# A kernel of attention and a Fourier layer: TensorE's operands at the right end of SBUF, helper tiles at the left, products with V in four blocks

## The chip, the cores and the metric

The kernel runs on one core of one Trainium2 chip. Its engines run side by side, each through its own list of instructions: TensorE (PE in the profile; PEld is its loading of weights, the stationary operand), VectorE (DVE), ScalarE (ACT), GpSimd (POOL), and SyncE (SP), which here issues every DMA. They wait for one another through semaphores. SBUF holds the tiles, PSUM the products of TensorE.

The metric is the time of one execution on the device in microseconds. Before the change it was 3028.86 us, the median of three runs (3026.84 to 3029.26).

## The reference, cut to what matters

Two layers on inputs of 2048 rows and 1024 columns, in float32; the results stand side by side in the output.

```python
def _A_ref(x, wqkv, wo):
    B, S, D = x.shape
    H = 32; Dh = D // H
    qkv = (x @ wqkv).reshape(B, S, 3, H, Dh).transpose(2, 0, 3, 1, 4)
    q, k, v = qkv[0], qkv[1], qkv[2]
    scores = jnp.einsum("bhqd,bhkd->bhqk", q, k) * Dh ** -0.5
    p = softmax(scores, axis=-1)
    o = jnp.einsum("bhqk,bhkd->bhqd", p, v)
    return o.transpose(0, 2, 1, 3).reshape(B, S, D) @ wo

def _B_ref(x, dft_seq_re, dft_seq_im, dft_hid_re, dft_hid_im):
    a = jnp.einsum("bsd,ed->bse", x, dft_hid_re)
    b = jnp.einsum("bsd,ed->bse", x, dft_hid_im)
    return jnp.einsum("ts,bse->bte", dft_seq_re, a) - jnp.einsum("ts,bse->bte", dft_seq_im, b)
```

## The kernel before, in words

**Dense products.** The products with wqkv, the two Fourier products and the one with wo (`qkv`, `dense1`, `dense2`, `project`) are each split in two by two blocks and done with seven block products instead of eight, from sums and differences of blocks. Each float32 operand is split into a high part (a cast, `halves`, L447 on VectorE or L445 on ScalarE) and the rest (a subtraction, L450), and three products (high with high, low with high, high with low) give one product's precision. So every dense product is a group of 12 or 24 matmuls at L361 in `group`, all in a type that TensorE takes in one pass. The stationary operand is a `piece` (tiles h and l) or, in `project` and in the V steps of `qkv`, a slot; the moving one is a slot of two halves of 512 columns (`moving`). What comes from memory lands in tiles raw and g (er in the early steps), is added up there (L425) and then split. A result is gathered from PSUM by VectorE, into a sum (an accumulator from `accs`, also a slot) or into tile e, and stored. Tile c brings back a stored partial result.

**Attention.** Head by head. `scores` computes q times k with 96 rows (L1162, 64 matmuls a head, out to psS), takes the row maximum on VectorE (L1168) and the exponential with its sum on ScalarE (L1171). `transposed` computes the transposed scores with 98 rows, the two extra carrying the row minimum of the negated maxima (L1285, 64 a head, out to psT), and ScalarE writes their exponentials into one of 27 tiles pt (L1289). Products with V (L1304) take the pt tiles of several key tiles at once, four column blocks of the array side by side; they are plain float32, two matmul instructions each. Up to which key tile a block of them goes is in ENDS: (0, 6, 11, 16), three blocks a head. `gather_o` (L1315, L1317) adds the blocks up, `result` scales them by tile rt and stores them.

**The order.** A planner written in the kernel (`Plan`) simulates the engines with fixed costs in microseconds and writes the order of all instructions out; the chip then keeps it. TensorE takes work of three streams of attention, S (L1162), T (L1285) and V (L1304), when it is ready, and otherwise a fill, the next matmul of a dense product. A fill goes ahead of attention only where the share of fills done lags behind the share of attention done (L1417, with RES fills held back). A product with V waits up to PATIENCE while other attention work is about to be ready or ScalarE has less than STOCK of work queued (L1392 to L1397). MM, PV and SWITCH are the planner's costs of a matmul, of one key tile in L1304 and of one switch to L1304 and back.

**Where tiles lie.** SBUF is allotted as two stacks that grow towards each other, one from the left end, the lowest addresses, and one from the right. Before the change:

- right: pool `big`, 20 slots of 4 KiB (0 to 19; the sums are 0 to 3 and 12 to 15 in the Fourier part), and pool `pre`, 21 tiles of 2 KiB (h, l, raw, g, e, c)
- left, one after another: `qk0` (qs0, ks0: q and k of even heads), `sm` (small tiles of the softmax), then `v` (early steps: er, sums of qkv, slots 28 to 31, vh, stage), which `att()` replaces by `att` (qs1, ks1, vt, qx, 27 pt, rt, ot), which `op_pool()` replaces by `op` (projection: slots 20 to 27, raw, g and kept tiles)

A pool allots its tiles in the order of their first use. Work that uses a pool's place after another waits for the last users of the former; `att_gate` collects the last work of the early qkv steps, and `behind` that of attention.

## Time and profile before

| | |
|---|---|
| median of three runs | 3028.86 us |
| the profiled execution | 3029.23 us |
| its span, first to last instruction | 3027.3 us |
| TensorE busy | 3002.2 us, 99% |
| VectorE busy | 2403.0 us, 79% |
| ScalarE busy | 2279.5 us, 75% |
| GpSimd busy | 849.6 us, 28% |
| granted TensorE clock, mean | 0.998 |

The profile records one execution. Busy times are from records of each instruction; a line such as `L361` is the line of the kernel. A group line gives the engine, the operation, what is written and read, shapes, how many there were, busy time and mean duration, then the idle time before them and what ended it. In a timeline each line has a start in us from the beginning of the span and a length; equal neighbours are merged with their count. Matmuls overlap in their pipeline and their ends are modelled, so the time that one costs is the distance between starts. A window line gives, for a stretch of time, the busy time and number of instructions of each engine asked for, the granted clock, the busy share of the DMA engines and GB/s.

### The profile page before, as it was taken

How to read it: one execution, taken by the hardware profiler on the slowest of the kernel's cores; microseconds unless marked ns; L12 is line 12 of the kernel's file. 1: busy time of each engine (PE TensorE's matmuls, PEld its weight loads, DVE VectorE, ACT ScalarE, POOL GpSimd, SP SyncE). 2: the span in 40 equal slices, each digit the busy share in tenths (PEclk: the TensorE clock that was granted, in tenths of full speed). 3: DMA queues.
4: the chain of work that ended last, by engine and by line, in shares of the span. 5: the costliest groups of instructions: out<-in, count | busy, mean ns of one | idle time of the engine just before them, and what ended most of it. 6: DMA issues, size and time to landing. Idle time of an engine off the chain costs nothing.

```text
span 3027.3 us, 45365 instructions
## 1 busy us (share of the span) xinstructions
PE 3002.2 (99%) x14912; PEld 2151.6 (71%) x14912; DVE 2403.0 (79%) x3243; ACT 2279.5 (75%) x4312; POOL 849.6 (28%) x631
## 2 busy tenths in 40 slices
PE   9999999999999999999999999999999999999999
PEld 7887666677677666777777666666666766776787
DVE  7778889788877877787777788887777789787896
ACT  4348888888888888888888788888888888885221
POOL 2313335132212321221112343332211254240142
PEclk9999999999999999999999999999999999999999
DMA  9975658666625644554535675555433586556852
GB/s 341 351 224 165 203 177 278 206 229 222 198 77 175 204 126 138 180 181 137 157 91 153 216 237 165 162 154 161 128 105 101 160 261 214 150 171 203 296 183 94
DMA packets 376313, 558.06 MB, mean 184 GB/s; under 512 B 110896, under 2 KB 110896, under 8 KB 376016
## 3 DMA queue, kind: packets, MB, share of 16 engines
q1 hardware_dynamic: 376080, 555.17, 57.6%
q8 instruction: 120, 1.97, 0.3%
q14 instruction: 113, 0.93, 0.1%
HBM read 401.93 MB, written 153.09 MB: 183 GB/s over the span
## 4 chain that ended last, share of the span: by engine, by line
PE 81%; DVE 3%; ACT 1%; DMA 1%; issue 1%; SPq 0%; DVEq 0%; ACTq 0%
PE pd L361 36%; PE psT L1285 15%; PE pd L1304 14%; PE psS L1162 14%; PE psT L361 3%; DVE negm L1168 1%; ACT psS L1171 1%; DVE raw L425 0%; DVE h L447 0%; DMA raw<-o_d 0%; DVE slot L447 0%; ACT pt L1289 0%; DMA out<-e 0%; DMA c<-u_d 0%; DMA g<-in_wd 0%
## 5 line engine op out<-in xcount | busy, mean ns | idle before, releaser
L1289 ACT ACTIVATE pt<-psT 128x512 f32<-128x512 f32 x2048 | 1178.0, 654 | 386.2 <-PE psT L1285 385.1
L1168 DVE TENSOR_REDUCE negm<-psS 128x1 f32<-128x1024 f32 x1024 | 1240.3, 1220 | 209.8 <-PE psS L1162 205.0
L1171 ACT ACTIVATE psS<-psS,negm 128x1024 f32<-128x1024 f32 x1024 | 1174.3, 1147 | 77.2 <-DVE negm L1168 73.2
L361 PE MATMUL pd<-slot,h 128*128 128x512 f32 x3352 | 1152.7, 394 | 0.0
L1285 PE MATMUL psT<-qs,ks 98*128 98x512 f32 x2048 | 816.3, 402 | 1.1 <-ACT pt L1289 1.1
L361 PEld LDWEIGHTS pd<-slot,h 128*128 128x128 f32 x3352 | 634.2, 189 | 141.9 <-issue 0.8
L361 PE MATMUL pd<-slot,l 128*128 128x512 f32 x1676 | 660.2, 394 | 0.5 <-DVE l L450 0.5
L1285 PEld LDWEIGHTS psT<-qs,ks 98*128 98x128 f32 x2048 | 385.1, 189 | 178.4 <-issue 74.6
L1162 PE MATMUL psS<-ks,qs 96*128 96x512 f32 x1552 | 482.0, 397 | 11.2 <-ACT psS L1171 9.5
L1304 PE MATMUL pd<-pt,vt 128*32 128x512 f32 x4096 | 462.1, 597 | 1.7 <-DVE slot L598 1.2
L450 POOL TENSOR_TENSOR l<-raw,h 128x512 fp32r<-128x512 f32 x150 | 201.4, 1343 | 902.6 <-DVE h L447 419.9
L425 POOL TENSOR_TENSOR raw<-raw,g 128x512 f32<-128x512 f32 x214 | 285.8, 1341 | 469.8 <-DMA raw<-in_ct 115.8
L361 PEld LDWEIGHTS pd<-slot,l 128*128 128x128 f32 x1676 | 317.3, 189 | 71.3 <-DVE l L450 0.9
L1162 PEld LDWEIGHTS psS<-ks,qs 96*128 96x128 f32 x1552 | 290.7, 189 | 86.2 <-ACT psS L1171 21.0
L1304 PEld LDWEIGHTS pd<-pt,vt 128*32 128x32 f32 x4096 | 123.5, 110 | 288.1 <-issue 270.3
L450 POOL TENSOR_TENSOR slot<-raw,slot 128x512 fp32r<-128x512 f32 x145 | 203.4, 1410 | 368.6 <-DVE slot L447 232.7
L1171 ACT ACTIVATION_READ_ACCUMULATOR psS<-psS,negm 128x1 f32 x1024 | 270.8, 264 | 0.0
L361 PE MATMUL pd<-slot,slot 128*128 128x512 f32 x768 | 195.5, 394 | 0.0
L361 PEld LDWEIGHTS pd<-slot,slot 128*128 128x128 f32 x768 | 144.4, 188 | 32.9
L447 DVE CAST h<-raw 128x512 fp32r<-128x512 f32 x321 | 153.2, 478 | 15.7 <-PE pd L361 13.5
L1162 PE MATMUL psS<-ks,qx 96*128 96x512 f32 x496 | 151.9, 397 | 0.3
L425 DVE TENSOR_TENSOR raw<-raw,g 128x512 f32<-128x512 f32 x158 | 121.8, 776 | 33.2 <-DMA raw<-in_ct 9.8
(116 smaller groups left out, 1852.1 us busy)
## 6 DMA issues: line engine op xcount, KB each, us to landing
raw<-in_ct SPq DMA_DIRECT2D x224, 256.0 KB
g<-in_ct SPq DMA_DIRECT2D x128, 256.0 KB
qk_d<-e SPq DMA_DIRECT2D x52, 512.0 KB
qs<-qk_d SPq DMA_DIRECT2D x128, 192.0 KB
ks<-qk_d SPq DMA_DIRECT2D x128, 192.0 KB
raw<-ab_d SPq DMA_DIRECT2D x96, 256.0 KB
c<-u_d SPq DMA_DIRECT2D x88, 256.0 KB
g<-ab_d SPq DMA_DIRECT2D x80, 256.0 KB
```

What stands on the lines that cost most here:

```text
L361: nc.tensor.matmul(box["ps"], a[1]((a[0].hi, a[0].lo)[u]()), b[1]((b[0].hi, b[0].lo)[v]()), start=k == 0, stop=k == n - 1)
L425: (nc.gpsimd if e == "POOL" else nc.vector).tensor_tensor(out=dest(), in0=dest() if a is None else a.get(), in1=other["q"] if "q" in other ...
L447: nc.vector.tensor_copy(hi(), raw())
L450: (nc.gpsimd if e == "POOL" else nc.vector).tensor_tensor(out=lo(), in0=raw(), in1=f(hi()), op=ALU.subtract)
L1162: nc.tensor.matmul(p[:, i * NB : i * NB + NB], (qx["t"] if own else QS[h % 2][0:96])[:, qt * P : qt * P + P], KS[h % 2][0:96, c * 1024 + i ...
L1168: nc.vector.tensor_reduce(out=ST["negm"][:, c, qt : qt + 1], in_=box["p"], axis=AX.X, op=ALU.max, negate=True)
L1171: nc.scalar.activation(box["p"], box["p"], AF.Exp, bias=ST["negm"][:, c, qt : qt + 1], accum_out=ST["sums"][:, c, qt : qt + 1])
L1285: nc.tensor.matmul(box["p"], KS[h % 2][0:98, t * P : t * P + P], QS[h % 2][0:98, j * NB : j * NB + NB], start=True, stop=True)
L1289: nc.scalar.activation(box["t"], box["p"], AF.Exp)
L1304: nc.tensor.matmul(po["p"][j * DH : j * DH + DH, :], VT[h][:, k, :], box["t"], start=(k == t0), stop=(k == t), tile_position=(0, j * DH),)
```

## The change

The slots and pools are dealt out anew, and the products with V are cut into four blocks.

- Right now: `big` with slots 0 to 11 alone, a new pool `parts` (h and l), `qk0`, in the early steps a pool `vh` (slots 28 to 39), in attention `att` (qs1, ks1, qx and 22 of the 27 pt), in the projection `oph` (slots 20 to 27).
- Left now: `pre` (raw, g, e, c), `sm`, in the early steps `v` (er, sums of qkv, the tiles vh, stage), from attention on `sums` (slots 12 to 19) with `atl` (5 of the pt, vt, rt, ot) above it, and `op` (raw, g, kept tiles) in the place of `atl`.
- The slots of moving tiles form a ring of 0 to 11 in place of 16 to 19 and 4 to 11; sums are 16 to 19 and 12 to 15. In the last two qkv steps the V weights and the x tiles have changed places between slots 0 to 3 and 16 to 19. Slots 12 to 19 come free with `att_gate`.
- ENDS is (0, 4, 8, 12, 16); MM, PV and SWITCH, RES and PATIENCE have other values; the small exponential of `sums` is worked in place (tile ww is gone).

```diff
-ENDS = (0, 6, 11, 16)
+NLOW = 5
+ENDS = (0, 4, 8, 12, 16)
...
     def slot(i, shape, dt=F32R):
-        if i >= 20:
-            return (vp if i >= 28 else op_pool()).tile(shape, dt, name=f"slot{i}")
-        return big.tile(shape, dt, name=f"slot{i}", tag=f"slot{i}")
-
-    pre = ctx.enter_context(tc.tile_pool(name="pre", bufs=1, side="right", reuse_waits="tile"))
+        if i < 12:
+            return big.tile(shape, dt, name=f"slot{i}", tag=f"slot{i}")
+        if i < 20:
+            att()
+            return late["sums"].tile(shape, dt, name=f"slot{i}", tag=f"slot{i}")
+        if i < 28:
+            op_pool()
+            return late["oph"].tile(shape, dt, name=f"slot{i}")
+        return vph.tile(shape, dt, name=f"slot{i}")
...
+    parts = ctx.enter_context(tc.tile_pool(name="parts", bufs=1, side="right", reuse_waits="tile"))
+    pre = ctx.enter_context(tc.tile_pool(name="pre", bufs=1, reuse_waits="tile"))
...
-    qk0 = tc.alloc_tile_pool(name="qk0", bufs=1)
+    qk0 = tc.alloc_tile_pool(name="qk0", bufs=1, side="right")
...
+    vph = tc.alloc_tile_pool(name="vh", bufs=1, side="right", reuse_waits="tile")
...
             vp.release()
-            late["att"] = a = tc.alloc_tile_pool(name="att", bufs=1, reuse_waits="tile")
+            vph.release()
+            late["sums"] = ctx.enter_context(tc.tile_pool(name="sums", bufs=1, reuse_waits="tile"))
+            late["atl"] = tc.alloc_tile_pool(name="atl", bufs=1, reuse_waits="tile")
+            late["att"] = a = tc.alloc_tile_pool(name="att", bufs=1, side="right", reuse_waits="tile")
...
-    AROUND, SUMS = (16, 17, 18, 19, 4, 5, 6, 7, 8, 9, 10, 11), (0, 1, 2, 3, 12, 13, 14, 15)
+    SUMS = (16, 17, 18, 19, 12, 13, 14, 15)
...
-    MM, PV, SWITCH, TINY = 0.234, 0.786, 0.515, 0.17
+    MM, PV, SWITCH, TINY = 0.229, 0.866, 0.19, 0.17
...
-    RES = 600
+    RES = 400
...
-    PATIENCE = 2.0
+    PATIENCE = 0.5
...
-                    box[key] = pre.tile([P, 4, P], F32R, name=key, tag=key, bufs=3)
+                    box[key] = parts.tile([P, 4, P], F32R, name=key, tag=key, bufs=3)
...
                 i = 8 * ((x + 1) % 2) + k
+                i = i if i < 12 else 20 + i
             else:
-                i = (8 * (x - 5) + k) % 12 if x < 11 or k < 4 else 8 + k
+                i = (8 * (x - 5) + k) % 12 if x < 11 else (16, 8)[k // 4] + k
...
-            WV[x, c] = moving((28 if x in (1, 3) else 12 if x == 10 else 16) + c, ...)
+            WV[x, c] = moving((28 if x in (1, 3) else 12 if x == 10 else 0 if x == 11 else 36) + c, ...)
...
                 for u in ahead[0].users + slots[28:]:
                     att_gate.extend(u)
+                for i in range(12, 20):
+                    slots[i] = list(att_gate)
...
-            B[x][n] = moving(AROUND[(8 * x + n) % 12], b_terms(p, n), ...)
+            B[x][n] = moving((8 * x + n) % 12, b_terms(p, n), ...)
...
         WHERE = {
-            1: ([16, 20], 0), 7: ([4, 8], 24), 2: ([0, 4], 20), 6: ([8, 0], 24),
-            5: ([4, 8], 20), 3: ([0, 4], 24), 4: ([8, 0], 20),
+            1: ([20, 24], 0), 7: ([4, 8], 20), 2: ([0, 4], 24), 6: ([8, 0], 20),
+            5: ([4, 8], 24), 3: ([0, 4], 20), 4: ([8, 0], 24),
         }
...
-            box["w"] = sm.tile([P, 2, NS], F32, name="ww", bufs=1)
-            nc.scalar.activation(box["w"], box["t"], AF.Exp)
+            nc.scalar.activation(box["t"], box["t"], AF.Exp)
...
+                here = pt_r.n % NPT < NLOW
...
-                    box["t"] = att().tile([P, NB], F32, name="pt", bufs=NPT)
+                    box["t"] = att_low().tile([P, NB], F32, name="ptl", bufs=NLOW) if here else att().tile([P, NB], F32, name="pt", bufs=NPT - NLOW)
```

30 lines of the change are left out of this document (17 added, 13 removed).

## The prediction

> **What bounds the kernel now.** I read the page first, engines and granted clock.
>
> ```profile
> span 3027.3 us, 45365 instructions
> PE 3002.2 (99%) x14912; PEld 2151.6 (71%) x14912; DVE 2403.0 (79%) x3243; ACT 2279.5 (75%) x4312; POOL 849.6 (28%) x631
> PEclk9999999999999999999999999999999999999999
> PE 81%; DVE 3%; ACT 1%; DMA 1%; issue 1%; SPq 0%; DVEq 0%; ACTq 0%
> ```
>
> TensorE is never without work, its clock is whole, and the chain that ended last is its own. So the question is how long one matmul takes, and whether anything slower hides behind TensorE. Busy time of a pipelined matmul doesn't tell that; starts do. In the timeline of the output projection (L361), the first product has its moving operand in slots 0 to 3 throughout; its stationary one lies in slots 16 to 19 (right stack) for four groups of 12, then in slots 20 to 23 (left stack).
>
> ```profile
> 2869.41 5.60 PE L361 MATMUL pd<-slot,slot 128*128 128x512 f32 x24
> 2874.85 5.68 PE L361 MATMUL psT<-slot,slot 128*128 128x512 f32 x24
> 2880.37 5.76 PE L361 MATMUL pd<-slot,slot 128*128 128x512 f32 x24
> 2885.97 5.76 PE L361 MATMUL psT<-slot,slot 128*128 128x512 f32 x24
> ```
>
> From start to start, the 24 with both operands on the right take 5.44 us, 226.7 ns each; the 24 with the weights on the left take 5.60 us, 233.3 each. Shape, moving tile and neighbours are the same: 6.6 ns go with where the weights lie. Two stretches without products with V, one of attention and one of the Fourier part alone behind it (windows of time: matmuls, weight loads, VectorE, ScalarE, GpSimd, granted clock, DMA share, GB/s):
>
> ```profile
> 815.42:841.47 26.05, 26.05 (x113) 21.17 (x112) 22.13 (x27) 25.31 (x48) 1.30 (x1) 1.00 0.35 96
> 2818.25:2849.56 31.31, 31.31 (x140) 25.90 (x138) 27.73 (x47) 7.54 (x12) 5.39 (x3) 1.00 0.86 311
> ```
>
> A window also counts one or two matmuls that run into it, so the first is 112 in 26.05 us, 232.6 ns, and the second 138 in 31.31 us, 226.9. In the second all operands (slots, h, l) lie on the right, while DMA is at 0.86 and VectorE at 27.73 of 31.31 us: traffic of others isn't what slows a matmul. In the first, 98-row (L1285) and 96-row (L1162) matmuls read qs, ks and qx from the left stack. Even few of these slow their neighbours; early, in a stream of fills from the right:
>
> ```profile
> 210.00 0.63 PE L1162 MATMUL psS<-ks,qs 96*128 96x512 f32 x2
> 210.47 0.40 PE L361 MATMUL pd<-slot,h 128*128 128x512 f32 x1
> 210.71 0.39 PE L361 MATMUL pd<-slot,l 128*128 128x512 f32 x1
> 210.94 0.62 PE L361 MATMUL pd<-slot,h 128*128 128x512 f32 x2
> 211.40 0.63 PE L1162 MATMUL psS<-ks,qs 96*128 96x512 f32 x2
> ```
>
> Two from the left and four from the right take 1.40 us, 233.3 each: one pair costs all six. So I read a step, not a sum: 226.7 where a stream reads from the right alone, about 233 where it touches the left.
>
> The second thing seen in the attention window is ScalarE: 25.31 of 26.05 us. Between products with V, attention goes at ScalarE's pace and the fills (Fourier and projection products) take what TensorE has left. A faster matmul alone doesn't shorten attention; it lets more fills run inside it.
>
> **The change, part by part.** *Placement.* How many matmuls change regime: windows by source line, attention from the first L1285 to the last product with V, and the end.
>
> ```profile
> 248.29:2817.90 2569.61, 1440.75 (x4869) 1.00 0.56 174
> 2880.37:3027.30 146.93, 142.97 (x613) 1.00 0.39 132
> ...
> 248.29:2817.90 2569.61, 816.34 (x2048) 1.00 0.56 174
> ...
> 71.68:248.29 176.61, 22.64 (x72) 1.00 0.76 260
> 248.29:2817.90 2569.61, 611.28 (x1976) 1.00 0.56 174
> ```
>
> (First two L361, the third L1285, the last two L1162.) Attention: 4869 + 2048 + 1976 = 8893 matmuls times 232.6 - 226.8 = 5.8 ns: 51.6 us. Projection: 613 x 6.6 ns = 4.0 us; its left slots become a right pool. Before attention: two V steps of 96 matmuls with slots 28 to 31 on the left, 1.3 us, and 36 pairs of L1162 that each hold back six, 36 x 6 x 6.6 ns = 1.4 us. What newly reads from the left are the last two steps of qkv, whose moving V weights (slots 12 to 15) and x tiles (16 to 19, 12 to 15) fall into the new left pool of sums: 8 + 8 + 16 groups of 12, 384 x 6.6 ns = 2.5 us back. Sum: 51.6 + 4.0 + 1.3 + 1.4 - 2.5 = 55.8 us off TensorE. No row shows a 96- or 98-row matmul reading from the right, so this has two ends: only the 128-row streams gain (5.3 us), or all do (55.8); I take the upper one, because a 128-row matmul shows the same 233 when its operand lies on the left.
>
> *Products with V in four blocks.* From 96 blocks of five or six key tiles to 128 of four.
>
> ```profile
> 2746.80 0.39 PE L361 MATMUL pd<-slot,h 128*128 128x512 f32 x1
> 2747.12 4.50 PE L1304 MATMUL pd<-pt,vt 128*32 128x512 f32 x40
> 2751.55 0.73 PE L1285 MATMUL psT<-qs,ks 98*128 98x512 f32 x2
> 2752.12 0.40 PE L361 MATMUL pd<-slot,h 128*128 128x512 f32 x1
> ...
> 2771.30 5.36 PE L1304 MATMUL pd<-pt,vt 128*32 128x512 f32 x48
> 2776.59 0.73 PE L1285 MATMUL psT<-qs,ks 98*128 98x512 f32 x2
> ```
>
> Five tiles hold TensorE 4.43 us, six 5.29: 0.86 a tile and 0.13 fixed. The entry takes 0.32 instead of 0.23, the two matmuls behind it 0.57 instead of 0.46. So a block costs 0.33 us beside its tiles, and 32 more cost 10.6 us on TensorE. Each brings one more add on VectorE:
>
> ```profile
> L1317 DVE TENSOR_TENSOR ot<-ot,pd 128x512 f32<-128x512 f32 x64 | 43.9, 687 | 122.3 <-PE pd L1304 122.1
> L598 DVE TENSOR_TENSOR slot<-slot,pd 128x512 f32<-128x512 f32 x12 | 8.2, 679 | 0.9 <-PE pd L361 0.8
> L598 DVE TENSOR_TENSOR acc<-acc,pd 128x512 f32<-128x512 f32 x10 | 6.8, 681 | 5.9 <-PE pd L361 5.7
> ```
>
> 32 x 0.687 = 22 us more on an engine with some 600 us idle: hidden while fills and scores go on in the other banks; uncovered it is at most 22 us. The lower two rows are the same add on the right (slot) and on the left (acc): 2 ns apart, so sums and raw tiles cost VectorE nothing on the left, and I put 0 there.
>
> The shorter block matters to ScalarE, which starves while one runs.
>
> ```profile
> ACT pt L1289 <- PE psT L1285: 385.1, 232, 6.0
> ```
>
> 385.1 us over 96 blocks is 4.0 each. A mean block with its entry is 16 x 0.86 / 3 + 0.13 + 0.32 = 5.04 us, one of four tiles 3.89; with the same stock of queued exponentials the starving falls by 1.15 to 2.85, and 128 x 2.85 = 365: attention becomes some 18 us shorter than its 2569.61.
>
> *The rest.* The share of fills held back (RES) and its slower rule don't bind: TensorE already ran ahead of that share, since fills fill whatever attention leaves. The new gate on slots 12 to 19 makes the first sum of the later qkv steps wait for the last early store; four free banks and the first scores lie over it, and I put 0, with 5 us if they don't cover it. DMA issues on SP keep number and size; exchanging slots 0 to 3 for 16 to 19 moves none past another. Working the small exponential in place removes no instruction. The planner's costs for a matmul, a tile of V and a switch decide the order alone; a plan nearer to 227 ns moves waits about, for which I allow the 2 us below.
>
> *Sum.* TensorE: 3029.23 - 55.8 + 10.6 = 2984.0. The profiled execution (3029.23) is 0.4 above the median 3028.86, which I neglect. Against it stands the end of attention:
>
> ```profile
> 2819.75 0.33 SPq L1334 DMA_DIRECT2D o_d<-ot  x1
> 2824.14 0.38 SPq L409 DMA_DIRECT2D raw<-in_wo  x1
> ...
> 2827.60 0.63 ACT L445 ACTIVATE slot<-raw 128x512 fp32r<-128x512 f32 x1 [16.83 <-DMA raw<-in_wo]
> ...
> 2866.69 2.88 PE L361 MATMUL psT<-slot,slot 128*128 128x512 f32 x12
> ...
> 3020.37 2.96 PE L361 MATMUL psT<-slot,slot 128*128 128x512 f32 x12
> ```
>
> Now 48.8 us of fills cover the way from the last product with V (2817.9) to the projection (2866.69). The saved time uses those up inside attention. The bare way is some 14 us by these rows (store, first weight load to cast 10 us, a few loads more). With 672 matmuls at 226.7 (152.3) and the tail behind the last (3027.3 - 3020.37 - 2.8 = 4.1) an attention of the old length ends at 2817.9 + 170.4 = 2988.3, 2990 with what lies around the span; 18 us shorter, it no longer binds. I take TensorE's sum and 2 us for waits that a faster TensorE meets: **2986 us**.
>
> **The rivals.**
>
> *Part of it stays left of the border.* On the right stack the rows show the fast regime down to 122 KiB from its end (20 slots of 4, 21 tiles of 2 KiB). After the change the stack is 138 KiB deep, and qs1 and ks1, allotted first in their pool, may lie lowest: 16 KiB that no row shows fast. If the border lies above them, odd heads stay slow, and L1285 of one head is mixed with L1162 of the next, so one of the two is always odd; the pair above spoils its six. Then between none and half of the 51.6 us comes: 3034 to 3009, nearer the former, 3028. For it: the unseen 16 KiB. Against: none of the fast rows weakens towards its low end (h and l lie lowest, 226.9).
>
> *Place does nothing for L1285 and L1162*; their row counts make the 233. Only 4.0 + 1.3 us come, and 10.6 are paid: 3034.5. Against it: the 128-row rows. The Trainium skill's page "SBUF — State Buffer" (Who interferes with whom) says that PE never waits on anyone and knows waits only at the port that VectorE and GpSimd share; by that rule placement is worth 0 altogether and the time would be 3029.2 + 10.6 = 3039.8. The trace disagrees, 226.7 against 233.3, so this has no chance beyond the rival's own.
>
> *ScalarE starves, slower.* The patience before a product with V falls from 2.0 to 0.5 us: a block may start before exponentials are queued, ScalarE loses up to 1.5 us a block, and fills run out before attention ends. It decides once attention ends later than 3027.3 - 170.4 = 2856.9, 57 us behind the 2800 expected, 0.44 us a block. With half of the 1.5: 2800 + 96 + 170.4 = 3066, 3068 with the rest. For it: 25.31 of 26.05. Against: with 16 of 27 exponential tiles in a block instead of 24, L1285 has eleven free ones to run ahead, so the stock refills itself.
>
> **How the numbers follow.** Forecast 0.70; border 0.12; place does nothing 0.06; starving 0.12. The forecast's own range is 2970 (attention and waits both shrink) to 3002 (attention not shorter, gate and added adds partly open). To leave out no more than 2 in 10 the range must take in the first two rivals: 2970 to 3036. A measurement tells 0.2%, 6 us. Faster: 0.70 and 0.04 of the border's 0.12: 0.74. Same: 0.05 of the border and 0.03 of the second: 0.08. Slower: the rest, 0.18.
>
> **What would show it.** Attention windows at about 227 ns a matmul for placement, odd and even heads alike; if the border is the cause, L1285 keeps two durations. L1304 in blocks of 32 holding about 3.57 us. ScalarE's wait for psT L1285 near 365 us; over 440 speaks for starving, with idle TensorE before the projection. Fewer than some 60 fills between the last product with V and the projection. It is wrong if matmuls stay at 232, or if TensorE falls below 98%.

## The result and the profile after

The changed kernel takes 3037.17 us (median of 7 runs, 3035.80 to 3040.12), the kernel before in the same runs 3029.26 (7 runs, 3026.84 to 3031.91). The ratio is 1.0026, with an interval from 1.0014 to 1.0038: slower by a quarter of a per cent. The forecast was 2986.

The page of the kernel changed: span, busy times, granted clock, and the engines' shares of the chain that ended last.

```profile
span 3034.8 us, 45369 instructions
PE 3010.0 (99%) x14912; PEld 2149.4 (71%) x14912; DVE 2435.1 (80%) x3283; ACT 2293.7 (76%) x4316; POOL 840.5 (28%) x619
PEclk9999999999999999999999999999999999999999
PE 92%; DVE 5%; ACT 1%; DMA 1%; issue 1%; POOL 0%; SPq 0%; ACTq 0%; DVEq 0%; POOLq 0%
```

TensorE still sets the end and its clock is whole in all 40 slices of the page, so the time must be looked for in the distance between matmuls again. The lines of the code have moved: L361 is L380 here, L1285 L1308, L1162 L1185, L1304 L1327, L1317 L1340, L1289 L1312. The timeline of the projection, all of whose operands lie on the right now (start, length, line, operation):

```profile
2881.04 5.60 PE L380 MATMUL pd<-slot,slot 128*128 128x512 f32 x24
2886.48 5.60 PE L380 MATMUL psT<-slot,slot 128*128 128x512 f32 x24
2891.92 5.60 PE L380 MATMUL pd<-slot,slot 128*128 128x512 f32 x24
```

Every 24 take 5.44 us, 226.7 ns each, where those with weights on the left had taken 5.60. That is what was expected. Two stretches of the attention without products with V, windows of time as before (matmuls, weight loads, VectorE, ScalarE, GpSimd, granted clock, DMA share, GB/s):

```profile
1228.95:1246.41 17.46, 17.46 (x76) 14.19 (x75) 16.84 (x23) 16.80 (x32) 9.40 (x7) 1.00 0.94 287
2561.48:2577.77 16.29, 16.29 (x71) 13.24 (x70) 15.85 (x20) 14.21 (x27) 9.32 (x7) 1.00 0.65 204
```

Both windows begin and end at a start, with one more matmul that runs into them: 75 in 17.46 us and 70 in 16.29 us are 232.8 and 232.7 ns. Nothing has been gained in the attention, although qs, ks, qx, h, l and the slots all lie on the right. The early fills with a pair of scores among them, in the timeline:

```profile
209.66 0.63 PE L1185 MATMUL psS<-ks,qs 96*128 96x512 f32 x2
210.12 0.39 PE L380 MATMUL pd<-slot,h 128*128 128x512 f32 x1
210.36 0.40 PE L380 MATMUL psT<-slot,h 128*128 128x512 f32 x1
210.59 0.40 PE L380 MATMUL psT<-slot,l 128*128 128x512 f32 x1
210.82 0.62 PE L380 MATMUL psT<-slot,h 128*128 128x512 f32 x2
211.28 0.40 PE L380 MATMUL psT<-slot,l 128*128 128x512 f32 x1
211.52 0.63 PE L1185 MATMUL psS<-ks,qs 96*128 96x512 f32 x2
```

Eight matmuls in 1.86 us, 232.5 each, with nothing read from the left. The pair still holds up its neighbours. What sets it apart from them is now its 96 rows alone.

A block of products with V in the timeline, one of 32 matmuls, with its entry and what follows it:

```profile
1543.81 0.39 PE L1308 MATMUL psT<-qs,ks 98*128 98x512 f32 x1
1544.13 3.64 PE L1327 MATMUL pd<-pt,vt 128*32 128x512 f32 x32
1547.70 0.73 PE L1308 MATMUL psT<-qs,ks 98*128 98x512 f32 x2
1548.27 1.09 PE L1185 MATMUL psS<-ks,qx 96*128 96x512 f32 x4
```

The add behind each block, among the costliest groups (busy time and mean ns of one):

```profile
L1340 DVE TENSOR_TENSOR ot<-ot,pd 128x512 f32<-128x512 f32 x96 | 65.9, 686 | 169.3 <-PE pd L1327 169.3
```

ScalarE's waits for the transposed scores, with their sum, number and longest (the tiles on the left have a name of their own now):

```profile
ACT pt L1312 <- PE psT L1308: 316.7, 235, 5.0
...
ACT ptl L1312 <- PE psT L1308: 59.1, 50, 3.6
```

And the last block of V, and SyncE's issue of the last store of the attention, in the timelines of TensorE and SyncE:

```profile
2841.02 3.64 PE L1327 MATMUL pd<-pt,vt 128*32 128x512 f32 x32
```
```profile
2846.87 0.33 SPq L1357 DMA_DIRECT2D o_d<-ot  x1
```

To say where 7.5 us of span went, all starts of the two traces were added up. Products with V with their entries hold TensorE 501.8 us instead of 488.8, 12.9 more before rounding, of which 32 x 0.232 = 7.4 are ordinary distances that would have stood there anyway. Distances over 250 ns between the other matmuls exceed the ordinary one by 44.3 us instead of 39.1, 5.2 more. The first matmuls behind the added blocks make 3.3 of these, so the fourth block costs 12.9 - 7.4 + 3.3 = 8.8 us. Another 4.9 arise where attention begins, between 240 and 300 us (7.4 us of such waits instead of 2.5), and elsewhere they are 3.0 fewer. At that beginning TensorE first sits idle for 1.33 and 0.58 us, waiting for ScalarE to free the scores' banks, and then has half its clock for some 9 us; the same stretch in windows, before and after:

```profile
255.00:264.00 9.00, 9.00 (x40) 7.30 (x39) 7.59 (x9) 9.00 (x19) 5.74 (x5) 1.00 0.75 241
255.00:264.00 9.00, 9.00 (x21) 6.51 (x22) 7.59 (x11) 8.37 (x16) 5.24 (x4) 0.50 0.63 206
```

The remaining 10,400 distances shrank from 232.19 to 231.88 ns, 3.3 us. Sum: 8.8 + 4.9 - 3.0 - 3.3 = 7.4 us slower. The blocks cost about what was forecast. The placement gave these 3.3 us of 55.8, if the new order has no part in them.

In what follows "the attention's mean" is the mean distance from start to start of two neighbouring one-pass matmuls (everything but the products with V) between the first and the last product with V, without distances over 250 ns, taken from all of some 8500 starts of a trace. Before it was 232.62 ns, after 232.83; the projection 233.33 and 226.67.

### The profile page after: what moved, and what is told of

Its sections match the earlier page's. It is cut to its first block, busy times and chain, and to the rows that moved or that the text cites. A ratio compares the mean times of both kernels' runs of the same rounds, so it can differ in the third digit from the quotient of the medians.

```text
span 3034.8 us, 45369 instructions
## 1 busy us (share of the span) xinstructions
PE 3010.0 (99%) x14912; PEld 2149.4 (71%) x14912; DVE 2435.1 (80%) x3283; ACT 2293.7 (76%) x4316; POOL 840.5 (28%) x619
## 4 chain that ended last, share of the span: by engine, by line
PE 92%; DVE 5%; ACT 1%; DMA 1%; issue 1%; POOL 0%; SPq 0%; ACTq 0%; DVEq 0%; POOLq 0%
PE pd L380 41%; PE psT L1308 15%; PE psS L1185 15%; PE pd L1327 14%; PE psT L380 7%; DVE negm L1191 2%; ACT psS L1194 1%; DVE slot L466 1%; DVE raw L444 1%; DVE slot L469 0%; DMA g<-in_ct 0%; DVE h L466 0%; DVE l L469 0%; DMA raw<-in_xb 0%; DVE e L896 0%
## 5 line engine op out<-in xcount | busy, mean ns | idle before, releaser
L1194 ACT ACTIVATE psS<-psS,negm 128x1024 f32<-128x1024 f32 x1024 | 1140.4, 1114 | 104.5 <-DVE negm L1191 98.5
L1312 ACT ACTIVATE pt<-psT 128x512 f32<-128x512 f32 x1668 | 940.0, 621 | 318.0 <-PE psT L1308 316.7
L380 PE MATMUL pd<-slot,h 128*128 128x512 f32 x3368 | 1168.0, 395 | 1.4 <-DVE h L466 1.4
L1308 PE MATMUL psT<-qs,ks 98*128 98x512 f32 x2048 | 815.3, 403 | 1.3 <-ACT pt L1312 1.3
L380 PEld LDWEIGHTS pd<-slot,h 128*128 128x128 f32 x3368 | 637.4, 189 | 156.8 <-issue 7.5
L380 PE MATMUL pd<-slot,l 128*128 128x512 f32 x1684 | 664.3, 394 | 0.0
L1308 PEld LDWEIGHTS psT<-qs,ks 98*128 98x128 f32 x2048 | 383.9, 189 | 187.5 <-issue 80.5
L1185 PE MATMUL psS<-ks,qs 96*128 96x512 f32 x1552 | 479.7, 398 | 5.9 <-ACT psS L1194 5.5
L1327 PE MATMUL pd<-pt,vt 128*32 128x512 f32 x3336 | 437.2, 596 | 1.3 <-DVE e L670 0.7
L469 POOL TENSOR_TENSOR l<-raw,h 128x512 fp32r<-128x512 f32 x137 | 186.4, 1361 | 825.0 <-PE psT L1308 297.6
L380 PEld LDWEIGHTS pd<-slot,l 128*128 128x128 f32 x1684 | 319.0, 189 | 76.1 <-issue 3.4
L1185 PEld LDWEIGHTS psS<-ks,qs 96*128 96x128 f32 x1552 | 291.7, 189 | 77.7 <-ACT psS L1194 15.5
L469 POOL TENSOR_TENSOR slot<-raw,slot 128x512 fp32r<-128x512 f32 x148 | 212.7, 1444 | 431.7 <-DVE slot L466 291.3
L1327 PEld LDWEIGHTS pd<-pt,vt 128*32 128x32 f32 x3336 | 108.5, 110 | 227.0 <-issue 212.9
L1312 ACT ACTIVATE ptl<-psT 128x512 f32<-128x512 f32 x380 | 219.1, 627 | 59.4 <-PE psT L1308 59.1
L1194 ACT ACTIVATION_READ_ACCUMULATOR psS<-psS,negm 128x1 f32 x1024 | 235.3, 230 | 0.0
L1340 DVE TENSOR_TENSOR ot<-ot,pd 128x512 f32<-128x512 f32 x96 | 65.9, 686 | 169.3 <-PE pd L1327 169.3
L380 PE MATMUL pd<-slot,slot 128*128 128x512 f32 x768 | 194.3, 391 | 0.2 <-DVE ot L1340 0.2
L380 PEld LDWEIGHTS pd<-slot,slot 128*128 128x128 f32 x768 | 144.3, 188 | 31.3 <-DVE ot L1340 0.6
```

What stands on the lines that cost most here:

```text
L380: nc.tensor.matmul(box["ps"], a[1]((a[0].hi, a[0].lo)[u]()), b[1]((b[0].hi, b[0].lo)[v]()), start=k == 0, stop=k == n - 1)
L469: (nc.gpsimd if e == "POOL" else nc.vector).tensor_tensor(out=lo(), in0=raw(), in1=f(hi()), op=ALU.subtract)
L1185: nc.tensor.matmul(p[:, i * NB : i * NB + NB], (qx["t"] if own else QS[h % 2][0:96])[:, qt * P : qt * P + P], KS[h % 2][0:96, c * 1024 + i ...
L1194: nc.scalar.activation(box["p"], box["p"], AF.Exp, bias=ST["negm"][:, c, qt : qt + 1], accum_out=ST["sums"][:, c, qt : qt + 1])
L1308: nc.tensor.matmul(box["p"], KS[h % 2][0:98, t * P : t * P + P], QS[h % 2][0:98, j * NB : j * NB + NB], start=True, stop=True)
L1312: nc.scalar.activation(box["t"], box["p"], AF.Exp)
```

## The experiments

**Rows.** First the row counts. For 128 rows the tiles of q and k get zeros in rows 96 to 127 (ones in rows 96 and 97 of k, as before). Rows 96 and 97 of q carry the minima for the transposed scores; from the third head on one more DMA a head zeroes them first, so that the scores for the maxima don't see those of an earlier head. The edit on the kernel changed (e1) and on the kernel before (e2):

```diff
-    QS, KS = [qk0.tile([98, S], F32R, name="qs0")], [qk0.tile([98, S], F32R, name="ks0")]
+    QS, KS = [qk0.tile([128, S], F32R, name="qs0")], [qk0.tile([128, S], F32R, name="ks0")]
+    nc.gpsimd.memset(f(QS[0])[96:128, :], 0.0)
+    nc.gpsimd.memset(f(KS[0])[96:128, :], 0.0)
...
+        if h > 1 and (which, j) == (0, 1):
+            nc.sync.dma_start(dst[96:98, NB:S], zero_d[:, NB:S])
...
-                        p[:, i * NB : i * NB + NB], (qx["t"] if own else QS[h % 2][0:96])[:, qt * P : qt * P + P],
-                        KS[h % 2][0:96, c * 1024 + i * NB : c * 1024 + i * NB + NB], start=True, stop=True,
+                        p[:, i * NB : i * NB + NB], (qx["t"] if own else QS[h % 2])[:, qt * P : qt * P + P],
+                        KS[h % 2][:, c * 1024 + i * NB : c * 1024 + i * NB + NB], start=True, stop=True,
...
-                    nc.tensor.matmul(box["p"], KS[h % 2][0:98, t * P : t * P + P], QS[h % 2][0:98, j * NB : j * NB + NB], start=True, stop=True)
+                    nc.tensor.matmul(box["p"], KS[h % 2][:, t * P : t * P + P], QS[h % 2][:, j * NB : j * NB + NB], start=True, stop=True)
```

> The changed kernel, with the scores' operands filled up to 128 rows of zeros, so that both kinds of score products (96 and 98 rows until now) are 128-row matmuls like the fills; three more small DMA columns a head set the two extra rows of q to zero. Theory A (a matmul with fewer than 128 rows slows itself and its neighbours wherever it reads): attention falls from 232 to about 227 ns a matmul, 8893 x 5 ns = 45 us, so 2990 us, or a little above if ScalarE sets the end of attention. Rival B (groups of a single matmul, each starting and stopping a sum in PSUM, are what slows): 232 ns stays, 3037 us. Rival C (the 16 KiB of qs1 and ks1 at the low end of the right stack): no change, 3037 us.

> The kernel before with the same filling up to 128 rows; q, k and the exponentials stay on the left. Theory A with the place as a second condition: a 128-row matmul that reads from the left costs 233 ns, so attention stays at 232 to 233 and the time within 3029 +- 6 us. Rival (rows alone decide, and place only in the projection): 227 ns in attention, 3029 - 45 = 2984 us.

Measured: e1 2995.65 us (0.9894 of before, 0.9881 to 0.9908), the attention's mean 227.80 ns; e2 3016.67 us (0.9961, 0.9948 to 0.9975), mean 231.53, projection 233.33. The windows of e1 whose first is the very stretch of 75 matmuls shown above of the kernel changed:

```profile
1210.22:1227.22 17.00, 17.00 (x76) 14.08 (x75) 15.88 (x21) 16.16 (x31) 8.44 (x7) 1.00 0.92 280
2547.49:2562.91 15.42, 15.42 (x70) 12.77 (x68) 14.00 (x24) 13.74 (x28) 6.91 (x5) 1.00 0.32 93
```

75 in 17.00 us are 226.7 ns. So the row counts were what kept the attention slow on the right, and they are worth 41.5 us there. With the old placement the same edit is worth 12.6, neither of the two values expected: something else holds the matmuls up there too.

**All at 98 rows (e6).** Is it fewer rows, or a change of their number from one matmul to the next? On e1:

```diff
-                    nc.tensor.matmul(box["ps"], a[1]((a[0].hi, a[0].lo)[u]()), b[1]((b[0].hi, b[0].lo)[v]()), start=k == 0, stop=k == n - 1)
+                    nc.tensor.matmul(box["ps"], a[1]((a[0].hi, a[0].lo)[u]())[0:98], b[1]((b[0].hi, b[0].lo)[v]())[0:98], start=k == 0, stop=k == n - 1)
```

(and 98 rows in the two kinds of scores. This kernel leaves out the last 30 of each 128 rows that a dense product sums over.)

> The run with 128-row scores on the right, but with every score product and every dense product at 98 rows: the dense products leave out rows 98 to 127 of each 128 they sum over. Theory A1 (fewer than 128 active rows slow a matmul): 233 ns a matmul everywhere, in the projection too, so 3040 us or more. Theory A2 (a change of the number of rows from one matmul to the next slows both): all rows equal, 227 ns everywhere as at 128, 2996 us.

2999.5 us in one run, mean 227.82, projection 226.67; a window of the attention:

```profile
2550.54:2565.96 15.42, 15.42 (x70) 12.76 (x68) 14.03 (x24) 13.75 (x28) 6.91 (x5) 1.00 0.32 92
```

The same 68 matmuls as in the second window of e1, 15.42 us in both. 98 rows throughout are as good as 128, by one run and its trace. It is the change of the number that costs.

**One kind of scores (e11).** e1 with the scores for the maxima back at 96 rows and the transposed ones at 128:

```diff
-                        p[:, i * NB : i * NB + NB], (qx["t"] if own else QS[h % 2])[:, qt * P : qt * P + P],
-                        KS[h % 2][:, c * 1024 + i * NB : c * 1024 + i * NB + NB], start=True, stop=True,
+                        p[:, i * NB : i * NB + NB], (qx["t"] if own else QS[h % 2])[0:96, qt * P : qt * P + P],
+                        KS[h % 2][0:96, c * 1024 + i * NB : c * 1024 + i * NB + NB], start=True, stop=True,
```

> The kernel changed, in which only the transposed scores (psT, 2048 matmuls) are computed over 128 rows and the scores for the maxima (psS, 2048 matmuls, in pairs) stay at 96. If each change of the number of rows between neighbours costs by itself, about half of them are gone: half of the 41.5 us between 3037.2 and 2995.65, near 3016 us, and the attention near 230.3 ns. If a stretch with any 96-row matmuls in it is slow as a whole, near 3037 us and 232.8 ns. If the 98 rows of psT alone were the trouble and 96 are well, near 2996 us.

3020.22 us (0.9967, 0.9955 to 0.9979), mean 230.91 ns: with some of the changes of row count gone, some of the time is gone, if less than the half expected.

**The parts of the change alone.** The placement with three blocks and the order's old numbers (e3), and four blocks with the new numbers on the old placement (e4):

```diff
-ENDS = (0, 4, 8, 12, 16)
+ENDS = (0, 6, 11, 16)
...
-    MM, PV, SWITCH, TINY = 0.229, 0.866, 0.19, 0.17
+    MM, PV, SWITCH, TINY = 0.234, 0.786, 0.515, 0.17
...
-    RES = 400
+    RES = 600
...
-    PATIENCE = 0.5
+    PATIENCE = 2.0
```

> The changed kernel with the blocks of before (three a head) and the planner's costs, RES and PATIENCE of before: placement alone. From the projection and two V steps 5.3 us of TensorE come, 2.5 go: 3026 us if the rest of the change is the blocks' doing; 3037 us if the placement itself costs what the change lost.

> The kernel before with four blocks a head and the new planner's costs, RES and PATIENCE: 32 blocks more at 0.33 us are 10.6 us on TensorE, so 3040 us. If ScalarE's shorter starving gave it back, 3029 us.

e3 3027.52 us (0.9997, 0.9988 to 1.0006), mean 232.69; e4 3043.48 (1.0051, 1.0039 to 1.0064). Placement alone cannot be told from no change; blocks and new numbers alone cost 15 us (0.0051 x 3029), 4 of them by a mean of 233.11 ns and 3 by waits where attention begins (5.8 us between 240 and 300 us). Those early waits go with the planner's numbers: the traces of every run with the new ones have 3.7 to 8.4 us of them, those with the old ones 2.5 to 2.8, in either placement, and the new ones with three blocks as with four (e10, e16). So there was hardly a gain of the placement that the blocks could have taken back.

**Three blocks at 128 rows.** e1 with the edit of e3 (e5), and with its first line alone (e10):

> The changed placement with 128-row scores, and the three blocks, planner's costs, RES and PATIENCE of before. If the parts add up: 2995.7 of the run with 128 rows on the right, less the 9.7 us by which placement alone (3027.5) lay under the whole change (3037.2): 2986 us. If ScalarE, starving 4 us a block, sets the end of attention instead: 2990 us or more.

> The kernel changed with 128-row scores and products with V in three blocks, everything else as in the changed kernel (its costs, reserve and patience of the hand-written order). With the costs, reserve and patience of the kernel before as well, three blocks gave 2996.75 us, at an attention of 228.8 ns a matmul instead of 227.8. If it was the order made by the old costs that kept more matmuls slow, the attention falls back to 227.8 ns and 16 us of blocks of V are saved: 2980 to 2986 us. If blocks of six themselves leave more slow matmuls behind, it stays at 228.8 ns and 2994 to 2999 us.

2996.75 us (0.9891, 0.9876 to 0.9906) with a mean of 228.78 ns, and 2995.06 (0.9885, 0.9868 to 0.9901) with 227.97. Neither is told apart from e1. Of three blocks, the products with V save 6.7 us of TensorE by the count above (14.0 less 32 x 0.227); in e10 longer waits (53.2 instead of 49.9 us) and a slower mean (10,425 x 0.15 ns = 1.6 us) leave 1.8. Expected had been 10 to 16.

**Start addresses, first try.** In e1's trace 384 one-pass products were still slow, with a mean of 232.8 ns: those that read slots 12 to 19, the only ones with an operand on the left. Besides lying left these slots start at another byte within 64 than what lies right (0 against 32), as everything on the left did in the kernel before. (Start addresses are those that the kernel's allotment gives the tiles, counted in bytes of a partition; no profile shows them.) Left stack of e2 moved up by 32 bytes (e7), right stack of e1 down by 32 (e8):

```diff
     const = ctx.enter_context(tc.tile_pool(name="const", bufs=1))
+    nc.gpsimd.memset(const.tile([P, 8], F32, name="shift"), 0.0)
```
```diff
+    shift = ctx.enter_context(tc.tile_pool(name="shift", bufs=1, side="right"))
+    nc.gpsimd.memset(shift.tile([P, 8], F32, name="shift"), 0.0)
     big = ctx.enter_context(tc.tile_pool(name="big", bufs=1, side="right"))
```

> The kernel before with 128-row scores and one unused tile of 32 bytes at the start of the left stack, so that all tiles there start 32 bytes past a multiple of 64, as those on the right already do (the right end lies 32 bytes below a multiple of 64). Theory P (the place decides: left slow, right fast): nothing changes against the run without it, 3017 us, projection at 233 ns. Rival Q (the start address within 64 bytes decides): everything becomes fast, projection 227 ns, about 2986 us, the run on the right with three blocks.

> The run with 128-row scores on the right, with one unused tile of 32 bytes at the right end, so that the tiles of the right stack start at multiples of 64 bytes. Theory P (place): nothing changes, 2996 us, 227 ns in the projection. Rival Q (start within 64 bytes): everything is slow, 233 ns, 10687 x 5.5 ns more, about 3050 us.

e7 3014.15 us (0.9948, 0.9933 to 0.9963), mean 231.48; e8 2996.09 (0.9892, 0.9875 to 0.9908), mean 227.77, the products with slots 12 to 19 as slow as before (233.0 ns where a slot is the moving operand, 231.1 where it is the stationary one). That seemed to settle it for the place. But the projection of e7 did not fit (L372 is the line of the dense products there):

```profile
2861.89 5.68 PE L372 MATMUL psT<-slot,slot 128*128 128x512 f32 x24
2867.41 5.76 PE L372 MATMUL pd<-slot,slot 128*128 128x512 f32 x24
2873.01 5.72 PE L372 MATMUL psT<-slot,slot 128*128 128x512 f32 x24
2878.57 5.66 PE L372 MATMUL pd<-slot,slot 128*128 128x512 f32 x24
2884.06 5.66 PE L372 MATMUL psT<-slot,slot 128*128 128x512 f32 x24
```

24 in 5.49 us at the end, 228.9 ns: neither 226.7 nor 233.3, after 32 bytes that changed no side.

**The mirror (e9).** e1 with both stacks exchanged, so that TensorE reads from the left and everything else lies right:

```diff
-    big = ctx.enter_context(tc.tile_pool(name="big", bufs=1, side="right"))
+    big = ctx.enter_context(tc.tile_pool(name="big", bufs=1))
...
-    pre = ctx.enter_context(tc.tile_pool(name="pre", bufs=1, reuse_waits="tile"))
+    pre = ctx.enter_context(tc.tile_pool(name="pre", bufs=1, side="right", reuse_waits="tile"))
...
-    qk0 = tc.alloc_tile_pool(name="qk0", bufs=1, side="right")
+    qk0 = tc.alloc_tile_pool(name="qk0", bufs=1)
```

(and so with the other pools.)

> The kernel changed with 128-row scores, with the two sides of SBUF exchanged: what TensorE reads lies in the lower half, raw tiles, results and sums in the upper. Its source, order and row counts are those of the run at 2995.65 us with TensorE's operands on the right. Theory A (an operand of the left half makes a one-pass matmul slow in itself): matmuls of the attention and of the projection near 233 ns, about 9500 x 6 = 57 us more than that run, so near 3050 us; at least the 3017 us of the kernel before with 128-row scores. Theory B (it is neighbouring matmuls, or the two operands of one, that must not lie on different halves): no matmul crosses any more than there, near 227.8 ns, so 2994 to 2999 us. In between, near 3015 us with the attention at 231.5 ns: only the scores' tiles on the left cost, and dense products read either side alike.

2997.24 us (0.9895, 0.9881 to 0.9910), mean 227.91, projection 226.67:

```profile
2546.70:2562.11 15.41, 15.41 (x69) 12.77 (x68) 14.01 (x24) 13.76 (x28) 6.90 (x5) 1.00 0.31 94
```

68 matmuls in 15.41 us, 226.6 ns, all from the left. The left half is not slow. Slow are, again, the products with slots 12 to 19, which now lie right, with means of 232.0 and 233.7 ns. In e1 slow and fast tiles start at 384 and 480 by the remainder after division by 512, in e9 at 480 and 384, in the kernel before at 0 and 480. A rule of not mixing what lies on two sides of a fixed border has another flaw: in e1 the border would have to lie below byte 88,032, where its fast tiles begin, and above its slow ones; but what e9 reads fast in its attention reaches from 384 to 96,640, across all of that.

**Equal remainders (e12 to e15).** The shift of e7 with 120 elements instead of 8 on e2, so that left and right operands all start at remainder 480 (e12); 24 elements on e1, which brings slots 12 to 19 to 480 (e13); 120 on the kernel before itself, scores at 96 and 98 rows (e14); 56 on e2, left at 224, right at 480 (e15):

```diff
     const = ctx.enter_context(tc.tile_pool(name="const", bufs=1))
+    nc.gpsimd.memset(const.tile([P, 120], F32, name="shift"), 0.0)
```

> The kernel before with 128-row scores (3016.67 us), with 480 bytes put at the bottom of the left stack and nothing else changed: the scores' tiles and slots 20 to 31 stay in the lower half, and the dense products' in the upper. With it every operand of TensorE starts at the same remainder by 512, 480, where the left ones were at 0 and the right ones at 480. Theory C (it is not the half but the remainder of the start addresses: matmuls whose operands, or whose neighbours' operands, differ in it are slow): attention 227 to 228.5 ns, projection 226.67 ns instead of 233.33, hence 3016.7 - 8400 x 3.7 ns - 600 x 6.7 ns = 2980 to 2986 us with three blocks, at most 2999. Theory B (the halves must not be mixed, whatever the remainder): attention 231.5, projection 228.9 to 233.3 ns, 3013 to 3017 us.

> The kernel changed with 128-row scores (2995.65 us), with 96 bytes put at the bottom of the left stack: slots 12 to 19, V's tiles and the five exponential tiles on the left then have the remainder 480 by 512 of everything on the right, where they had 384. Theory C: the 384 products whose moving slot is one of 12 to 19 fall from 233 to 227 ns, and those after a block of V too: attention 227.0 to 227.3 ns instead of 227.8, 2.5 to 7 us less, so 2989 to 2993 us. Theory B: they lie on the left as before, 233 ns, and 2995 to 2997 us.

> The kernel before itself (scores over 96 and 98 rows) with 480 bytes put at the bottom of the left stack, one line. Theory C with the cost of changing the number of rows, which the kernel changed shows at equal remainders (232.8 ns in the attention, 226.67 in the projection): attention near 232.8 as it is, projection 226.67 ns (4.1 us off), early steps 1 to 2 us off, so 3022 to 3025 us. Theory B: 3027 to 3031 us, projection 228.9 to 233.3 ns.

> The kernel before with 128-row scores, with 224 bytes at the bottom of the left stack: left operands at remainder 224, right ones at 480, 256 apart. If theory C holds and equality within 128 or 256 bytes is what counts, as the run with 480 bytes: projection 226.67, attention 227 to 228.5 ns. If it must be equal within 512 bytes, the projection stays near 229 to 233 ns and the attention near 231.5, 3013 to 3017 us.

e12 2991.19 us (0.9878, 0.9862 to 0.9895), mean 228.67; e13 2991.96 (0.9879, 0.9864 to 0.9894), mean 227.41; e14 3024.34 (0.9984, 0.9975 to 0.9994), mean 232.64; e15 2990.70 (0.9871, 0.9852 to 0.9891), mean 228.79; the projection 226.67 in all four. The same stretch of 104 matmuls, which the order of these kernels keeps, in one window each, first of the kernel before:

```profile
2184.25:2208.44 24.19, 24.19 (x106) 19.65 (x104) 20.48 (x26) 24.08 (x46) 2.61 (x2) 1.00 0.49 137
```

of e2 (128 rows, 32 bytes apart):

```profile
2177.73:2201.80 24.07, 24.07 (x105) 19.52 (x104) 20.46 (x26) 23.98 (x46) 2.58 (x2) 1.00 0.50 138
```

of e14 (96 and 98 rows, equal):

```profile
2185.02:2209.19 24.17, 24.17 (x106) 19.65 (x104) 20.43 (x26) 24.07 (x46) 2.58 (x2) 1.00 0.48 138
```

and of e12 (128 rows, equal):

```profile
2160.15:2183.90 23.75, 23.75 (x105) 19.52 (x104) 20.42 (x25) 23.69 (x46) 2.58 (x2) 1.00 0.48 140
```

Without the one or two that run into them they hold 104 matmuls each, in 24.19, 24.07, 24.17 and 23.75 us: neither cure alone does much, both together do. (The first 49 of e12 take 11.11 us, 226.7 ns each; what slows the rest is taken up under e16.) The main finding of the study, by whole runs, all with the old placement and three blocks:

| | scores at 96 and 98 rows | scores at 128 rows |
|---|---|---|
| left operands 32 bytes apart from right ones | 3027 to 3030 us (before) | 3016.67 us (e2) |
| same remainder everywhere | 3024.34 us (e14) | 2991.19 us (e12) |

No tile has changed sides in this table. The single cures bring 12 and 4 us, both together 37. In e13 the products with slots 12 to 19 fell from between 231 and 235 to between 226 and 229 ns where they lie, on the left.

**How far equality must go (e17), and the converse (e18).** e2 with 88 elements, left at 352, right at 480, 128 apart; and e1 with 32 bytes put into the right stack, after which qs, ks, qx, pt and slots 20 to 27 start at 448, h, l and slots 0 to 11 at 480, all on the right:

```diff
+    gap = ctx.enter_context(tc.tile_pool(name="gap", bufs=1, side="right"))
+    nc.gpsimd.memset(gap.tile([P, 8], F32, name="gap"), 0.0)
     qk0 = tc.alloc_tile_pool(name="qk0", bufs=1, side="right")
```

> The kernel before with 128-row scores and 352 bytes at the bottom of the left stack: left operands at remainder 352, right ones at 480, 128 apart. 64 apart was slow (attention 231.5, projection 228.9 ns), 256 apart as fast as equal. If equality within 128 bytes is what counts: projection 226.67, attention 228.7 ns, near 2991 us. If within 256: projection 228 to 234, attention 231.5 ns, 3013 to 3017 us.

> The kernel changed with 128-row scores (2995.65 us), with one tile of 32 bytes put into the right stack ahead of the pool of qs0 and ks0. All that TensorE read in the upper half it still reads there, but qs, ks, qx, the exponential tiles and the projection's slots 20 to 27 then start at remainder 448, h, l and slots 0 to 11 at 480: 32 bytes apart, as in the kernel before. Theory C: the kernel before's slow steps come back inside one half: projection 233.3 ns (4 us), attention 231.5 ns (8500 x 3.7 ns = 31 us), so 3027 to 3032 us. Theory B (halves): 227.8 and 226.67 ns, 2994 to 2998 us.

e17 3015.48 us (0.9954, 0.9938 to 0.9970), mean 231.20. e18 3034.01 us (1.0014, 1.0005 to 1.0024), mean 231.87, 38 us more than e1 for one tile of 32 bytes. The stretch of 75 matmuls that took 17.00 us in e1 is shown behind its projection's timeline (L392 is the line of the dense products there):

```profile
2873.60 5.76 PE L392 MATMUL pd<-slot,slot 128*128 128x512 f32 x24
2879.20 5.76 PE L392 MATMUL psT<-slot,slot 128*128 128x512 f32 x24
2884.80 5.76 PE L392 MATMUL pd<-slot,slot 128*128 128x512 f32 x24
```

And the stretch in a window:

```profile
1225.41:1242.80 17.39, 17.39 (x77) 14.07 (x75) 17.07 (x23) 16.80 (x32) 9.42 (x7) 1.00 0.97 308
```

5.60 us for 24 again, 233.3 ns, with all operands on the right, and 17.39 us for the 75, 231.9 ns. Unequal remainders are enough. With the projection as the gauge: 32 bytes apart 233.3 ns, 64 apart 228.9, 128 apart 232.4, equal or 256 apart 226.7. As far as these distances tell, what must be equal is the start address modulo 256; 256 apart itself is one run, e15.

**A better order on equal remainders (e16).** e12 with the last three edits of e3 turned round (the changed kernel's costs, reserve and patience):

> The fast run with halves mixed and equal remainders (2991.19 us: the kernel before, 128-row scores, 480 bytes at the bottom of the left stack), with the planner's costs, reserve and patience of the kernel changed, three blocks of V kept. On the right those numbers of the order took the attention from 228.8 to 228.0 ns a matmul with three blocks. If they do the same here: 8450 x 0.7 ns = 6 us less, 2984 to 2987 us. If other waits take it back: 2989 to 2993 us.

2989.89 us (0.9873, 0.9858 to 0.9888), mean 227.53. The mean fell by 1.1 ns, 9.6 us over 8500; waits over 250 ns grew from 43.7 to 51.1 us and ate most of it.

Why an order changes the mean can be read from the traces. A weight load mostly starts 2 to 4 ns behind the matmul ahead of it; call it late from 12 ns on. Take only the distances that have no late load, block of V or distance over 250 ns among the ten matmuls ahead of them: their means are 226.9 ns in e12 and 226.7 in e16, but 231.4 in e2, 232.4 in e14 and 232.5 in the kernel before. There, with both causes gone, nothing slow is left. The other distances have means of 230.5 ns in e12 and 230.4 in e16; e12 has 4176 of them, e16 1961. In e12, 89 of the 100 late loads that open such a slow stretch are those of transposed scores, which wait for ScalarE to free their bank; in e16 it is 5 of 13. So what is left of slow matmuls goes with late weight loads ahead of them. That these are the cause is argued from the order of events; no run varied them alone.

e16 has the lowest median of the study and isn't told apart from e12, e13 and e15; each beats both kernels, by 36 us or more.

## Why the prediction was wrong, step by step

*What bounds the kernel.* Right: TensorE, by the distance of its starts. The reading "a step, not a sum: 226.7 where a stream reads from the right alone, about 233 where it touches the left" was right as to its two values and wrong as to what they go with. Left and right stack differed in one more thing, the remainder of their start addresses, and no row of the kernel before could tell the two apart, since every left operand had 0 and every right one 480. The prediction's own sign of being wrong, matmuls that stay at 232, is what the windows of after show.

*Placement, 55.8 us.* This step failed, in the choice "I take the upper one, because a 128-row matmul shows the same 233 when its operand lies on the left". That one cause gives 233 does not exclude a second that gives the same 233 where the first is gone. Two ends were named, 5.3 and 55.8, though the lower left out the 2.5 us back and should have been 2.8; the run fell there: 3.3. The projection (4.0) came as worked out, since the right stack has one remainder throughout; the 96- and 98-row matmuls among 128-row ones kept the attention at 232.8. The early pair, read as a proof of place, was a proof of either. Removing row changes as well brought 41.5 us on the right (e1), so most of the time looked for was there, for another edit.

*Four blocks, 10.6 us.* Right in mechanism and near in size: 0.32 before the block (1543.81 to 1544.13), 3.57 for it, 0.57 behind it, and 8.8 us by all starts.

*The rest.* "2 us for waits" was the allowance for another plan; the waits where attention begins alone grew by 4.9, with the clock at 0.50 in the stretch shown. They go with the planner's numbers by the runs. The gate on slots 12 to 19, put at 0, cost nothing that shows: e3 and e5 have it, and 2.6 and 2.8 us of waits there against 2.5 before.

*Adds on VectorE, 0.* L1340 ran 96 times at 686 ns, 32 more than before. VectorE's busy time rose by 32 us, 22 of them these adds, on an engine with 600 us idle; no experiment took the adds alone away.

*ScalarE starving.* 316.7 + 59.1 = 375.8 us, 2.94 a block against 2.85 forecast and 365 in sum (385.1 less 365 is 20, not 18). But "attention becomes some 18 us shorter" did not come: the last block of V started at 2841.02, and the store of its result was issued at 2846.87, 27 us later than before. Fills between it and the projection were 147 matmuls instead of 211, not under 60. The gain in starving was to be paid out by a faster TensorE, which wasn't there.

*Border.* Falls already by the trace of after: qs0 and ks0, 151,520 bytes up and more, are as slow as qs1 and ks1 below them (means of 233.9 ns at L1308 for both heads). e1 reads the same tiles fast, down to byte 88,032: the stack's depth plays no part.

*Place does nothing for L1285 and L1162*, the rival with 3034.5 us and a chance of 0.06, is what happened on the right, 2.7 us from the time; its sum left out the 2.5 us back, and with them it gives 3037.0. That this meets 3037.17 is partly luck: the sum has no early waits and 10.6 for blocks that cost 8.8. The rival had deserved more: nothing in the profile spoke against it but rows that speak for a second cause. In the kernel before row counts were one of two causes, as e2 and e12 show.

*ScalarE starves, slower* did not come: TensorE stayed at 99%, and the chain that ended last at 92% TensorE.

The Trainium skill's page "SBUF — State Buffer" (Who interferes with whom), by which PE waits on no one, was put aside in the prediction on the strength of 226.7 against 233.3. That was a misreading, since these two differ by start addresses and not by what other engines do. The trace agrees with the page: e1's two windows go at 226.7 and 226.8 ns at DMA shares of 0.92 and 0.32. The section "Operand start alignment" of the same page of the Trainium skill says that an operand must start at a multiple of its element size; every kernel here keeps that, and e18's 32 bytes still cost 38 us, so the rule is one of validity and tells nothing of the time.

What stays open: the first matmuls behind a block of V are slow in every kernel (in e12 the second to fifth have means of 233.5, 231.8, 233.6 and 230.5 ns, from the twelfth 226.7), perhaps because the products with V use another number of columns; that wasn't tried. Nor were late weight loads. Unequal remainders cost between neighbours (e2, where both operands of a score are at 0 and both of a dense product at 480). Whether they also cost within one matmul isn't shown: in the projection of the kernel before the weights differ from the moving tile of their own matmul and from that of its neighbours alike. Why a change of either kind costs anything no run shows.

## What to carry to other kernels

Where one matmul takes 3% longer than another of the same shape, vary one thing at a time before moving anything: a tile of 480 bytes, one line, did what a new map of SBUF was meant to do, and 128 rows instead of 96 and 98 did the rest. Two causes that each give the same slow value hide one another: curing one shows little, so undo them together and then singly. When a forecast rests on the choice between a lower and an upper end, the row to ask for is one in which only the feature in question differs.

## What the runs showed of the hardware

- One-pass matmuls of 128 x 512 follow one another every 226.7 ns when the operands of neighbours start at the same address modulo 256 and use the same number of rows (226.7 to 226.9 in e12 and e16, away from blocks of V and late weight loads), and mostly every 231 to 234 ns when either differs; both defects together are hardly worse than one (232.6 against 231.5 and 232.6).
- The half of SBUF makes no difference (226.6 ns from the left in e9, 226.7 from the right in e1).
- Fewer rows cost nothing if all have them: 68 matmuls in 15.42 us at 98 rows and at 128.
- 64 bytes apart is a middle case for the projection (228.9 ns) and none for the attention (231.5).
- Behind a weight load that starts late, several matmuls go at some 232 ns even when both are equal (in e12 the first distance has a mean of 232.6, and 226.7 is reached again some ten to twenty matmuls on); that the load is the cause is argued, not tested.
- Where TensorE had sat idle for 1.33 and then 0.58 us at the start of attention, waiting for ScalarE, the kernel changed had a clock of 0.50 from 255 to 264 us, with 21 matmuls where the kernel before had 40 at 1.00.
